# Windowed attention and a dense layer on one core: the two heads of an outer tile side by side in 384 columns, and four blocks for the global queries

## The chip, the core and the metric

The kernel runs on one core of a Trainium2 chip. The metric is the device time of one execution in microseconds (us), the median of several runs. The profile and the trace come from one more execution, which the hardware profiler recorded; its times stand beside its own span and not beside the median. PE is the TensorE matmul engine and PEld its weight load, DVE is VectorE, ACT ScalarE, POOL GpSimd, and SP the SyncE, whose queue issues nearly all DMAs here.

## The reference

For 8 batches of 8 heads with 512 local and 32 global tokens of 64 values, local queries see the global keys and the local keys at most 32 positions away; global queries see all 544 keys. The result goes through a dense layer of 512 to 768 to 512 with the maximum of three products in the middle.

```
out_g = softmax(scale * q_g @ [k_g, k_l].T) @ [v_g, v_l]
s_ll  = where(|i - j| <= 32, scale * q_l @ k_l.T, -1e9)
out_l = softmax([scale * q_l @ k_g.T, s_ll]) @ [v_g, v_l]
x = concat(out_g, out_l) as (8 * 544, 512)
out = maximum(maximum(x @ w1, x @ w2), x @ w3) @ w_out
```

All is float32. Where the kernel needs its exactness at the fast matmul form (float32r), a value is split into a high part (a cast) and a low part (a subtraction), and products of the parts are added.

## The kernel before

The two heads of a pair go together: 8 batches of 4 pairs make 32 pairs (`p`), and each pair has four tiles (`t` = 0 to 3) of 128 local queries, so there are 128 tiles. A tile `sl` = 4p + t sees one window of keys out of a list of 18 groups of 32 (the 16 local ones and twice the global one, `UNITS`): 192 keys for t = 0 and 3, which are the outer tiles, and 224 for t = 1 and 2 (`WIN`).

The loop at L567 handles one tile in each pass, in stages that lie some passes apart: `scores` three tiles ahead (L315: matmuls into PSUM, mask, exponential, division by the sum; the weights `s` then go to the tile `prob` by a DMA, L351, from tile 16 on), `trans` one tile ahead (L354: transposes on PE by an identity into the one PSUM bank `turned`, which the trace calls T, then a copy into `pt`, and from tile 26 on also a subtraction for the low part), and `pv` for the tile itself (L391: matmuls with the values). Between these, `fill(n)` puts in n matmuls of the dense layer for the batch before (`moe_local`, lines L441 and L462), so that PE has work while a tile's softmax passes through DVE, ACT and POOL. At a batch's start `fill(400)` finishes the layer of the batch two back.

Before, `s` and `prob` are laid out as two heads of 256 columns. `trans` makes four transposes: for each head one of 128 keys (L362) and one of the rest, 64 or 96 (L363). The copy reads all 512 columns of T.

Global queries: `glob` (L274) computes the 64 rows of the pair's two heads against 544 keys a pair ahead, `glob_soft` (L297) normalises them into `sg` and sends them in six pieces by DMA (`GPUT`, L303) into `probg`, three blocks of 128 keys. Each tile then transposes one block (`transg`, L381) and copies 64 or 128 of its columns behind the 128 local queries of `pt`, so that the same `pv` matmuls treat them: such a matmul has 160 columns for each of the two parts, 320 in all, in place of 256. With 64 or 128 columns copied, the number of wide matmuls over t = 0, 1, 2, 3 is 2, 4, 2, 4. For pairs 0 to 3 (whose tiles are the first 16, in the order `SEQ`) the global queries come later, in `late` (L496), one pair in the course of every four tiles from 16 to 31; it loads keys and values again into `side`, makes six transposes, multiplies them by a mask `cover`, and adds up twelve small matmuls.

The first 16 tiles (`EARLY`) use plain float32 and the tile `early` without a DMA; the weights of the dense layer are unpacked from their 64-bit form at the same time (`convert`, on ACT, DVE and POOL).

The order on each engine is set by a scheduler, which takes the program in the order in which it is written and moves instructions by their dependences. Which engine does a copy or a subtraction is chosen by `least`, from running sums of estimated costs, so a change in widths can move such work between engines.

Of the kernel before, what the change touches and what calls it, by code (L numbers as in the profile page):

```python
# [33 lines left out]
for _o, _w in WIN:  # L34
# [20 lines left out]
def body(ctx, tc, kin, qin, vin, min_, win, out):  # L55
# [73 lines left out]
    early = const.tile([128, 4, 2, 256], F32, name="early", tag="early")  # L129
# [167 lines left out]
    def glob_soft(p):  # L297
        if p >= B * NP:
            return
        s, nm, z = pg[p]  # L300
        soft(s, nm, z)
        for c0, n, i, h, d0 in GPUT:
            nc.sync.dma_start(out=f32(probg[p % 2])[64 * h:64 * h + 64, i, d0:d0 + n], in_=s[:, c0:c0 + n])  # L303
# [10 lines left out]
    def scores(sl):  # L314
# [26 lines left out]
        for j in range(2):  # L341
            dve.tensor_tensor_reduce(out=s[:, j, 0:n], in0=ph[j][:, 0:n], in1=mask[:, (1, 0, 1, 0)[t], 32 * (t == 0):32 * (t == 0) + n],  # L342
                                     scale=-0.125, scalar=3.0e38, op0=ALU.add, op1=ALU.min, accum_out=nm[:, j:j + 1])
            act.activation(out=s[:, j, 0:n], in_=s[:, j, 0:n], func=AF.Exp, bias=nm[:, j:j + 1], scale=-1.0,  # L344
                           accum_out=z[:, j:j + 1])
        for j in range(2):
            dve.tensor_scalar(out=z[:, j:j + 1], in0=z[:, j:j + 1], scalar1=1e-9, scalar2=None, op0=ALU.add)  # L347
            dve.reciprocal(out=z[:, j:j + 1], in_=z[:, j:j + 1])
            times(s[:, j, 0:n], s[:, j, 0:n], z[:, j:j + 1])
        if sl >= EARLY:  # L350
            nc.sync.dma_start(out=f32(sc[sl])[:, :, 0:n], in_=s[:, :, 0:n])  # L351
        spend("d", 2 * (n * 1.04 + 75) + 150)
        spend("a", 2 * (n * 0.833 + 278))

    def trans(sl):
# [3 lines left out]
        ps, n = turned, WIN[sl % 4][1] - 128  # L359
        pr, ident = (ps, one) if sl < EARLY else (ps.bitcast(F32R), identr)  # L360
        for j in range(2):
            pe.transpose(pr[:, 256 * j:256 * j + 128], s[:, j, 0:128], ident)  # L362
            pe.transpose(pr[0:n, 256 * j + 128:256 * j + 256], s[:, j, 128:128 + n], ident)  # L363
        src = ps.rearrange("p (x q) -> p x q", q=128)
        if sl < NAT:
            pt = pts[sl] = att.tile([128, 2, 2, 160], F32, name="pt", tag="pt")
            copy(pt.rearrange("p j c q -> p (j c) q")[:, :, 0:128], src, True)
        else:
            pt = pts[sl] = att.tile([128, 2, 2, 2, 160], F32R, name="pt", tag="pt")
            v = pt.rearrange("p j c a q -> p (j c) a q")  # L370
            copy(v[:, :, 0, 0:128], src, True)
            sub(v[:, :, 1, 0:128], src, f32(v)[:, :, 0, 0:128], True)

    def transg(sl):
# [4 lines left out]
        i, h, n = GCH[t]  # L379
        g = psS.tile([128, 512], F32, name="S")  # L380
        pe.transpose(g.bitcast(F32R)[:, 0:128], probg[p % 2][:, i], identr)  # L381
# [305 lines left out]
```

## Time and profile before

| | us |
|---|---|
| median of 3 runs | 829.01 |
| lowest and highest of the runs | 828.31, 830.57 |
| the profiled execution's own time | 830.49 |
| its span, first to last instruction | 828.7 |
| PE busy in the span | 803.0 |
| DVE, ACT, POOL busy | 614.8, 510.2, 459.3 |

The profile counts how long each engine was busy and shows by which wait it stood. Matmuls are pipelined: one lasts longer than the distance to the next, so what a PE instruction costs in a dense stretch is read from the starts of its successors in the timeline, not from its duration. On SP, a row is the time in which the queue issues a DMA; the data land later.

### The profile page before, as it was taken

Reading aid. Unit: us, or ns where it says so; the run is one execution under the profiler, and the core shown is the slowest. Engines: PE = TensorE matmul, PEld = TensorE weight load, DVE = VectorE, ACT = ScalarE, POOL = GpSimd, SP = SyncE. Lnnn points to the kernel's source line nnn. Section 1 sums busy time; section 2 is a strip of 40 time slices with the busy share of each in tenths; the row PEclk is TensorE's granted clock in tenths of the full one; section 3 lists DMA queues with packets and bytes.
Section 4 is the critical chain, followed back from the end, with each engine's and each line's share of the span. In section 5 each row is a group of like instructions: output and inputs, shape, how many; then the busy total and the mean of one; then the engine's idle time right before and its main releaser. Section 6 shows DMA issues by size and latency. Waiting matters only on the chain.

```text
span 828.7 us, 16580 instructions
## 1 busy us (share of the span) xinstructions
PE 803.0 (97%) x4772; PEld 683.8 (83%) x4772; DVE 614.8 (74%) x2192; ACT 510.2 (62%) x1416; POOL 459.3 (55%) x623
## 2 busy tenths in 40 slices
PE   6788999999999999999999999999999999999997
PEld 5577888888888888888888888888888888888896
DVE  6999997878887888888887888788887888412111
ACT  5888786666666666666766667676666666311111
POOL 3223355756676667767675676866776665311211
PEclk9989999999999999999999999999999999999999
DMA  8956555533335333443335333443335332100001
GB/s 295 314 178 224 169 152 149 165 116 99 116 108 152 112 97 104 131 136 94 99 104 170 112 98 97 127 139 98 97 96 165 110 100 63 60 13 1 25 27 26
DMA packets 97466, 98.15 MB, mean 118 GB/s; under 512 B 19296, under 2 KB 85856, under 8 KB 97376
## 3 DMA queue, kind: packets, MB, share of 16 engines
q1 hardware_dynamic: 97232, 96.87, 38.0%
q8 instruction: 38, 0.62, 0.3%
q14 instruction: 52, 0.43, 0.2%
q10 hardware_dynamic: 144, 0.23, 0.1%
HBM read 60.39 MB, written 8.91 MB: 84 GB/s over the span
## 4 chain that ended last, share of the span: by engine, by line
PE 80%; DVE 5%; DMA 4%; issue 3%; ACT 3%; POOL 3%; SPq 1%; POOLq 0%; ACTq 0%; DVEq 0%
PE pm L441 45%; PE pm L462 16%; PE O L409 6%; PE S L339 5%; PE T L362 2%; PE T L363 2%; DMA prob<-s 2%; PE S L289 1%; PE S L335 1%; POOL h L103 1%; PE O L401 1%; DMA vraw<-v_in 1%; ACT s L344 1%; PE S L381 1%; DMA raw<-w_in 1%
## 5 line engine op out<-in xcount | busy, mean ns | idle before, releaser
L441 PE MATMUL pm<-xs,w 128*128 128x512 f32 (+1 forms) x2160 | 487.3, 366 | 1.3 <-ACT m L115 0.9
L441 PEld LDWEIGHTS pm<-xs,w 128*128 128x128 f32 x2160 | 354.3, 190 | 52.7 <-issue 4.2
L462 PE MATMUL pm<-w,h 128*128 128x512 f32 x612 | 157.5, 397 | 2.3 <-POOL h L103 2.1
L103 POOL TENSOR_TENSOR h<-m,h 128x512 fp32r<-128x512 f32 (+1 forms) x59 | 70.3, 1192 | 108.5 <-ACT h L115 107.9
L462 PEld LDWEIGHTS pm<-w,h 128*128 128x128 f32 x612 | 109.0, 188 | 23.0 <-POOL h L103 4.4
L450 DVE TENSOR_TENSOR m<-pm,m 128x512 f32<-128x512 f32 (+1 forms) x120 | 72.8, 607 | 66.3 <-PE pm L441 65.6
L103 POOL TENSOR_TENSOR qs<-qraw,qs 128x256 fp32r<-128x256 f32 x100 | 76.7, 767 | 70.4 <-issue 34.8
L344 ACT ACTIVATE s<-s,nm 128x192 f32<-128x192 f32 (+1 forms) x224 | 103.3, 462 | 19.6 <-DVE nm L342 14.1
L125 POOL TENSOR_SCALAR s<-s,z 128x224 f32<-128x224 f32 (+1 forms) x192 | 83.9, 444 | 36.1 <-ACT lox L115 20.4
L342 DVE CUSTOM_DVE_ANT_0 s<-S,mask 128x192 f32<-128x192 f32 (+1 forms) x224 | 74.5, 369 | 15.2 <-PE S L339 7.0
L103 DVE TENSOR_TENSOR pt<-T,pt 128x512 fp32r<-128x512 f32 x102 | 70.4, 690 | 19.4 <-ACT pt L115 18.2
L103 POOL TENSOR_TENSOR vs<-vraw,vs 128x256 fp32r<-128x256 f32 x102 | 75.6, 741 | 12.6 <-ACT vs L115 9.3
L409 PEld LDWEIGHTS O<-pt,vs 128*128 128x128 f32 x408 | 66.2, 188 | 9.9 <-issue 1.6
L409 PE MATMUL O<-pt,vs 128*128 128x320 f32 (+1 forms) x408 | 72.9, 300 | 1.4 <-DVE pt L103 1.4
L339 PEld LDWEIGHTS S<-kst,qs 128*128 128x128 f32 x400 | 59.5, 190 | 8.7 <-DVE nmg L293 0.2
L417 DVE TENSOR_TENSOR xr<-O,lox 64x160 f32<-64x160 f32 x204 | 64.4, 315 | 3.1
L103 POOL TENSOR_TENSOR kst<-kraw,kst 64x576 fp32r<-64x576 f32 x44 | 63.9, 1453 | 4.3 <-DMA prob<-s 1.0
L115 ACT CAST pt<-T 128x512 fp32r<-128x512 f32 x102 | 60.3, 591 | 9.5 <-PE T L363 7.1
L115 ACT CAST qs<-qraw 128x256 fp32r<-128x256 f32 x94 | 38.3, 407 | 44.0 <-PE S L339 28.8
L115 ACT CAST h<-m 128x512 fp32r<-128x512 f32 (+1 forms) x59 | 33.2, 562 | 51.7 <-DVE m L450 51.6
L339 PE MATMUL S<-kst,qs 128*128 128x192 f32 (+1 forms) x400 | 59.5, 270 | 0.0
L347 DVE TENSOR_SCALAR z<-z 128x1 f32<-128x1 f32 x256 | 37.5, 147 | 27.1 <-ACT s L344 17.9
(123 smaller groups left out, 1183.7 us busy)
## 6 DMA issues: line engine op xcount, KB each, us to landing
vraw<-v_in SPq DMA_DIRECT2D x122, 128.0 KB, 2.3
qraw<-q_in SPq DMA_DIRECT2D x100, 128.0 KB, 2.2
prob<-s SPq DMA_DIRECT2D x56, 224.0 KB, 2.5
raw<-w_in SPq DMA_DIRECT2D x24, 512.0 KB, 5.3
prob<-s SPq DMA_DIRECT2D x56, 192.0 KB, 2.3
out_dram<-o SPq DMA_DIRECT2D x32, 256.0 KB, 2.4
kraw<-k_in SPq DMA_DIRECT2D x25, 320.0 KB, 3.1
qn<-q_in SPq DMA_DIRECT2D x29, 128.0 KB, 3.6
```

The lines of the kernel that those rows point to most:

```text
L103: (dve if least(c) == "d" else pool).tensor_tensor(out=out, in0=a, in1=b, op=ALU.subtract)
L115: act.copy(out=out, in_=a)
L125: pool.tensor_scalar(out=out, in0=a, scalar1=col, scalar2=1.0, op0=ALU.mult, op1=ALU.mult)
L339: pe.matmul(ph[j][:, 0:n], lhsT=qs[sl][:, a, 128 * j:128 * j + 128], rhs=kst[p][:, j, c0:c0 + n], start=(a == 0), stop=(a == 1))
L342: dve.tensor_tensor_reduce(out=s[:, j, 0:n], in0=ph[j][:, 0:n], in1=mask[:, (1, 0, 1, 0)[t], 32 * (t == 0):32 * (t == 0) + n], scale=-0.12 ...
L344: act.activation(out=s[:, j, 0:n], in_=s[:, j, 0:n], func=AF.Exp, bias=nm[:, j:j + 1], scale=-1.0, accum_out=z[:, j:j + 1])
L347: dve.tensor_scalar(out=z[:, j:j + 1], in0=z[:, j:j + 1], scalar1=1e-9, scalar2=None, op0=ALU.add)
L409: pe.matmul(o[:, j, 0:320].rearrange("p (a q) -> p a q", a=2)[:, :, 0:n], lhsT=vs[sl][:, 2 * j + c].rearrange("p a d -> p (a d)"), rhs=pt[ ...
L417: dve.tensor_tensor(out=xr[p][64 * j:64 * j + 64, t], in0=o[0:64, j, 0:160], in1=lo[:, j], op=ALU.add)
L441: pe.matmul(ps[:, 0:n], lhsT=weight(3 * f + i, w)[:, 128 * k:128 * k + 128], rhs=xs[k][:, a, c0:c0 + n], start=(q == 0), stop=(q == 11))
L450: dve.tensor_tensor(out=m[:, 0:n], in0=ps[:, 0:n], in1=m[:, 0:n], op=ALU.max)
L462: pe.matmul(ps, lhsT=hh[f][:, a, 128 * t:128 * t + 128], rhs=weight(18 + f, w), start=(q == 0), stop=(q == 17))
```

## The change

Outer tiles keep the weights of the two heads side by side, 192 columns each, so 384 in all. `trans` then makes three transposes of 128: keys 0 to 127 of the first head, the last 64 of the first with the first 64 of the second, and the rest of the second. The values are packed on the host to fit: a head's part of a shared block meets zeros in the other head's rows. `pv` makes as many matmuls as before (four to a tile, or four of the high and low kind); copies and subtractions of `pt` have 384 columns for outer tiles and 512 for inner ones. Inner tiles keep four transposes, in another order of blocks.

`probg` has four blocks, one for each tile, filled by ten DMAs in place of six; seven of the ten have 32 rows, the others 64 as all had before. The number of 32-column pieces copied behind `pt` becomes 3, 4, 2, 3 for the four tiles (96, 128, 64 and 96 columns; before 64, 128, 64 and 128), and the number of wide `pv` matmuls 3, 4, 2, 4. `late` has its own value array `vg` of 640 columns (before 1024 columns of `v`), five transposes in place of six, ten small matmuls in place of twelve, and a plain copy in place of the multiplication by `cover`, which is gone with its six memsets.

```diff
-GPUT = [(0, 128, 0, 0, 0), (128, 96, 1, 0, 32), (224, 96, 1, 1, 0), (320, 64, 0, 1, 64), (384, 96, 2, 0, 32),
-        (480, 64, 2, 1, 0)]
+GPUT = [(0, 32, 0, 128, 0, 0, 0), (32, 32, 0, 64, 0, 32, 64), (32, 32, 64, 64, 0, 64, 0),
+        (0, 64, 128, 96, 1, 0, 32), (0, 64, 224, 96, 1, 64, 0), (0, 64, 320, 64, 2, 0, 64),
+        (0, 32, 384, 96, 3, 0, 32), (0, 32, 480, 64, 3, 32, 0), (32, 32, 384, 32, 3, 32, 96), (32, 32, 416, 128, 3, 64, 0)]
-GCH = [(0, 0, 1), (1, 0, 2), (0, 1, 1), (2, 0, 2)]
+GBL = [3, 4, 2, 3]
...
-        for c0, n, i, h, d0 in GPUT:
-            nc.sync.dma_start(out=f32(probg[p % 2])[64 * h:64 * h + 64, i, d0:d0 + n], in_=s[:, c0:c0 + n])
+        for r0, m, c0, n, i, e0, d0 in GPUT:
+            nc.sync.dma_start(out=f32(probg[p % 2])[e0:e0 + m, i, d0:d0 + n], in_=s[r0:r0 + m, c0:c0 + n])
...
+        if sl >= EARLY and outer(sl):
+            nc.sync.dma_start(out=f32(sc[sl])[:, 0:2 * n], in_=whole[:, 0:2 * n])
...
+    def outer(sl):
+        return sl % 4 in (0, 3)
+    def block(sl, j, c):
+        return j + c if outer(sl) else 2 * c + j
...
-        for j in range(2):
-            pe.transpose(pr[:, 256 * j:256 * j + 128], s[:, j, 0:128], ident)
-            pe.transpose(pr[0:n, 256 * j + 128:256 * j + 256], s[:, j, 128:128 + n], ident)
+        x = 3 if outer(sl) else 4
+        if x == 3:
+            for b in range(3):
+                pe.transpose(pr[:, 128 * b:128 * b + 128], s[:, 128 * b:128 * b + 128], ident)
...
-        g = psS.tile([128, 512], F32, name="S")
-        pe.transpose(g.bitcast(F32R)[:, 0:128], probg[p % 2][:, i], identr)
+        pe.transpose(g.bitcast(F32R)[:, 0:128], probg[p % 2][:, t], identr)
...
+    def wide(t, j, c):
+        return c == 0 or t in (1, 3) or (t == 0 and j == 1)
...
-                    n = 160 if c < GCH[t][2] else 128
+                    b = block(sl, j, c)
+                    n = 160 if wide(t, j, c) else 128
...
-    PARTS = [(0, 0, 0), (1, 0, 96), (1, 1, 224), (2, 0, 256), (3, 0, 352), (3, 1, 480)]
+    PARTS = [0, 128, 256, 384, 416]
...
-        dve.tensor_tensor(out=gt, in0=g[:, 0:384].rearrange("p (x g) -> p x g", g=64), in1=cover.to_broadcast([128, 6, 64]), op=ALU.mult)
+        copy(gt, g[:, 0:320].rearrange("p (x g) -> p x g", g=64), True)
```

The lines of the changed kernel have other numbers: L371 are the three transposes of an outer tile, L393 the transpose of the global block, L338 the scores, L425 the `pv` matmuls, L457 the dense layer; L299 the `probg` DMAs, L350 and L352 the `prob` DMAs of an outer and an inner tile.

On PE, this is one pass of the loop in the middle of the program, with the transposes of an outer tile (T from `prob`), before:

```order
L441 MATMUL pm<-xs,w_396 128x512 x10
L381 MATMUL S<-identr,probg 128x128
L362 MATMUL T<-identr,prob 128x128
L363 MATMUL T<-identr,prob 64x128
L362 MATMUL T<-identr,prob 128x128
L363 MATMUL T<-identr,prob 64x128
L441 MATMUL pm<-xs,w_437 128x512 x4
L339 MATMUL S<-kst,qs 128x224 x4
```

and now:

```order
L457 MATMUL pm<-xs,w_392 128x512 x10
L393 MATMUL S<-identr,probg 128x128
L371 MATMUL T<-identr,prob 128x128 x3
L457 MATMUL pm<-xs,w_432 128x512 x4
L338 MATMUL S<-kst,qs 128x224 x4
```

The neighbours and their counts are the same; three transposes of full width stand where two full and two half ones stood.

On SP, this is the stretch from a `probg` burst to the second `prob` DMA after it, for a pair in the middle of a batch (`prob1` is for the tile with t = 1, `prob0` for t = 2; `sg` is what the burst sends), before:

```order
L227 DMA kraw_6838<-k_in 128x640
L303 DMA probg1_96<-sg_6605 64x128
L303 DMA probg1_96<-sg_6605 64x96 x2
L303 DMA probg1_96<-sg_6605 64x64
L303 DMA probg1_96<-sg_6605 64x96
L303 DMA probg1_96<-sg_6605 64x64
L250 DMA qraw_6829<-q_in 128x256
L351 DMA prob1_94<-s_6727 128x2x224
L265 DMA vraw_6873<-v_in 128x256
L250 DMA qraw_6915<-q_in 128x256
L351 DMA prob0_93<-s_6808 128x2x224
```

and now:

```order
L299 DMA probg0_95<-sg_6942 32x128
L299 DMA probg0_95<-sg_6942 32x64 x2
L299 DMA probg0_95<-sg_6942 64x96 x2
L299 DMA probg0_95<-sg_6942 64x64
L352 DMA prob1_94<-s_7063 128x2x224
L299 DMA probg0_95<-sg_6942 32x96
L299 DMA probg0_95<-sg_6942 32x64
L299 DMA probg0_95<-sg_6942 32x32
L299 DMA probg0_95<-sg_6942 32x128
L246 DMA qraw_7168<-q_in 128x256
L261 DMA vraw_7212<-v_in 128x256
L246 DMA qraw_7254<-q_in 128x256
```

`prob1` now stands behind six `probg` issues, where six and a `qraw` stood before it; the other four, `qraw`, `vraw` and a second `qraw` stand between it and `prob0`.

On SP at the first pair of a batch (where the stores `out_dram` of the dense layer are issued too), before:

```order
L303 DMA probg0_95<-sg_7584 64x128
L303 DMA probg0_95<-sg_7584 64x96 x2
L303 DMA probg0_95<-sg_7584 64x64
L303 DMA probg0_95<-sg_7584 64x96
L303 DMA probg0_95<-sg_7584 64x64
L250 DMA qraw_7817<-q_in 128x256
L265 DMA vraw_7859<-v_in 128x256
L351 DMA prob1_94<-s_7710 128x2x224
```

and now:

```order
L299 DMA probg0_95<-sg_7598 32x128
L299 DMA probg0_95<-sg_7598 32x64 x2
L299 DMA probg0_95<-sg_7598 64x96 x2
L299 DMA probg0_95<-sg_7598 64x64
L299 DMA probg0_95<-sg_7598 32x96
L299 DMA probg0_95<-sg_7598 32x64
L299 DMA probg0_95<-sg_7598 32x32
L352 DMA prob1_94<-s_7723 128x2x224
L299 DMA probg0_95<-sg_7598 32x128
```

Here nine `probg` issues stand before `prob1`, where six, a `qraw` and a `vraw` stood.

More of the change, by code (lines that the diff above doesn't have):

```diff
@@ L128, in body @@
     make_identity(nc, one)
-    early = const.tile([128, 4, 2, 256], F32, name="early", tag="early")
+    early = const.tile([128, 4, 512], F32, name="early", tag="early")
     identr = const.tile([128, 128], F32R, name="identr")
@@ L134, in body @@
     dve.memset(zero, 0.0)
-    prob = [const.tile([128, 2, 256], F32R, name=f"prob{i}") for i in range(2)]
-    probg = [const.tile([128, 3, 128], F32R, name=f"probg{i}") for i in range(2)]
+    prob = [const.tile([128, 512], F32R, name=f"prob{i}") for i in range(2)]
+    probg = [const.tile([128, 4, 128], F32R, name=f"probg{i}") for i in range(2)]
     qgz = const.tile([128, 2, 160], F32R, name="qgz")
-    cover = const.tile([128, 6, 1], F32, name="cover")
     def clear():
-        pool.memset(cover, 1.0)
-        for x, a, n in ((1, 0, 32), (2, 96, 32), (3, 0, 64), (4, 0, 32), (5, 64, 64)):
-            pool.memset(cover[a:a + n, x], 0.0)
         for t in (*probg, qgz):
@@ L322, in scores @@
         else:
-            s = att.tile([128, 2, 224], F32, name="s")
+            s = att.tile([128, 448], F32, name="s")
             sc[sl] = prob[sl % 2]
+        w = n if outer(sl) else 256 if sl < EARLY else n
+        whole = s
+        s = [s[:, w * j:w * j + n] for j in range(2)]
         nm = small.tile([128, 2], F32, name="nm")
@@ L399, in pv @@
             for c, j in ((0, 0), (0, 1), (1, 0), (1, 1)):
-                n = 160 if sl >= EARLY and c < GCH[t][2] else 128
-                pe.matmul(o[64 * j:64 * j + 64, 0, 0:n], lhsT=vraw[sl][:, 2 * j + c], rhs=pt[:, j, c, 0:n], start=(c == 0), stop=(c == 1))
+                b = block(sl, j, c)
+                n = 160 if sl >= EARLY and wide(t, j, c) else 128
+                pe.matmul(o[64 * j:64 * j + 64, 0, 0:n], lhsT=vraw[sl][:, 2 * j + c], rhs=pt[:, b, 0:n], start=(c == 0), stop=(c == 1))
             n = 160 if sl >= EARLY else 128
@@ L661, in _pack @@
                     m[np.abs(d) <= 32, t - 1, 32 * c + i] = 0.0
-    return k, q, v, m
+    once = UNITS[:12] + UNITS[13:]
+    vg = np.concatenate([vt[u][0] for u in once[:16]] + [zero[0]] * 3 + [vt[once[16]][0]], axis=1)
+    vg = np.ascontiguousarray(vg.reshape(NP, 2, 5, 128, D).transpose(0, 3, 2, 1, 4)).reshape(NP, 128, 640)
+    return k, q, v, vg, m
 def _pieces(w1, w2, w3, w4):
```

73 lines of the change are left out of this document (43 added, 30 removed).

## The prediction

> **What bounds the kernel now.** I read the page's busy times first, then stretches of the span, then who waited for whom on PE once the first stage is over.
>
> ```profile
> PE 803.0 (97%) x4772; PEld 683.8 (83%) x4772; DVE 614.8 (74%) x2192; ACT 510.2 (62%) x1416; POOL 459.3 (55%) x623
> ```
> ```profile
> 38.00:42.00 4.00, 1.79 (x16) 1.11 (x15) 4.00 (x13) 3.70 (x10) 0.00 (x0) 1.00 0.88 297
> 42.00:46.00 4.00, 2.78 (x8) 1.74 (x9) 4.00 (x14) 3.20 (x9) 2.21 (x2) 0.54 0.02 6
> 46.00:50.00 4.00, 4.00 (x22) 3.99 (x21) 4.00 (x15) 3.72 (x12) 0.70 (x1) 0.61 0.04 5
> ```
> ```profile
> 125.00:150.00 25.00, 22.62 (x212) 20.41 (x211) 19.65 (x80) 16.33 (x48) 14.10 (x21) 1.00 0.54 155
> ...
> 451.00:543.00 92.00, 91.45 (x515) 77.99 (x513) 76.27 (x275) 61.92 (x173) 63.16 (x88) 1.00 0.39 117
> ...
> 724.00:829.00 105.00, 100.05 (x543) 86.85 (x541) 16.93 (x32) 15.52 (x30) 16.34 (x17) 0.99 0.06 18
> ```
> ```profile
> PE pm L462 <- POOL h L103: 2.1, 4, 0.5
> PE T L362 <- DMA prob<-s: 0.5, 2, 0.3
> ```
>
> A row of the stretches has the start and end, the length, then busy us of PE, PEld, DVE, ACT and POOL, the granted clock, the DMAs' share and their GB/s. There are three stages. Up to about 150 us PE has holes, and DVE is full (4.00 of 4 us in all three short rows): weights are unpacked there. From 180 to 724 us, where the last two rows hold, PE is full; it waits 2.6 us in all. The last 105 us are the dense layer alone, which the change doesn't touch. So an instruction taken from PE in the middle stage is worth its distance to the next one, and work taken from DVE, ACT or POOL there is worth nothing.
>
> **Transposes: the gain.** These are an inner tile's transposes (first one, and the matmul after the fourth), and all rows of an outer tile.
>
> ```profile
> 457.08 0.23 PE L362 MATMUL T<-identr,prob 128*128 128x128 f32 x1
> ...
> 457.37 1.15 PE L441 MATMUL pm<-xs,w 128*128 128x512 f32 x4
> ```
> ```profile
> 462.84 0.22 PE L381 MATMUL S<-identr,probg 128*128 128x128 f32 x1
> 462.89 0.23 PE L362 MATMUL T<-identr,prob 128*128 128x128 f32 x1
> 462.96 0.23 PE L363 MATMUL T<-identr,prob 128*64 128x128 f32 x1
> 463.02 0.24 PE L362 MATMUL T<-identr,prob 128*128 128x128 f32 x1
> 463.10 0.23 PE L363 MATMUL T<-identr,prob 128*64 128x128 f32 x1
> 463.16 1.14 PE L441 MATMUL pm<-xs,w 128*128 128x512 f32 x4
> ```
>
> From first start to the next matmul, four transposes cost 0.27 us in the outer tile (384 columns of weights) and 0.29 in the inner one (448 columns). If that is a fixed part for each of four and a part for each column, 64 columns cost 0.02, the 384 columns 0.12, and the fixed part is (0.27 - 0.12) / 4 = 0.04. Three transposes of 128 then cost 0.27 - 0.04 = 0.23. By the distance after a full-width one (0.07 and 0.08) they cost about 0.22. I take a saving of 0.05 us for each outer tile. The bounds: three at 0.08 save 0.03; three at 0.05, the distance from the global transpose to the next, save 0.12; at columns alone, nothing (a rival below). From tile 32 on there are 48 outer tiles, so 48 x 0.05 = 2.4 us; tiles 16 to 31 have 8, 0.4 us. In the first 16 PE isn't full, and I count that below.
>
> Copies and subtractions of `pt` get shorter by 128 columns on ACT and DVE. In the middle stage that is hidden work, 76.27 and 61.92 busy of 92; worth nothing.
>
> **Wide matmuls: the loss.** A pair has 13 wide `pv` matmuls for 12.
>
> ```profile
> L409 PE MATMUL O<-pt,vs 128*128 128x320 f32 x306 | 66.9, 307 | 1.4 <-DVE pt L103 1.4
> ...
> L409 PE MATMUL O<-pt,vs 128*128 128x256 f32 x102 | 27.6, 279 | 0.0
> ```
>
> The fixed part of a duration is the same in both, so the 64 more columns cost 28 ns, once in each of the 24 pairs from tile 32 on: 0.7 us lost.
>
> **The late global queries.** For one of the four pairs, first its transposes and the next instruction, then its twelve small matmuls (24 instructions, since plain float32 goes in two) and the next:
>
> ```profile
> 101.95 0.58 PE L513 MATMUL S<-one,side 64*128 64x64 f32 x6
> 102.46 0.76 PE L401 MATMUL O<-pt,vraw 128*64 128x160 f32 x8
> ...
> 104.36 0.89 PE L519 MATMUL O<-gt,side 128*64 128x32 f32 x24
> 105.18 0.26 PE L363 MATMUL T<-identr,prob 128*96 128x128 f32 x1
> ```
>
> A transpose costs 0.51 / 6 = 0.09, the matmuls 0.82 / 24 = 0.034 each, and one and four go: 0.22 us a pair, 0.9 in all if PE were full. It idled 2.4 us of 25 in one stretch of this stage, so I take 0.7, between 0 and 0.9.
>
> **The first stage.** There DVE and ACT matter.
>
> ```profile
> L515 DVE TENSOR_TENSOR gt<-S,cover 128x384 f32<-128x384 f32 x4 | 2.2, 546 | 0.0
> ```
> ```profile
> L115 ACT COPY pt<-T 128x512 f32<-128x512 f32 x24 | 14.0, 582 | 4.4 <-PE T L363 4.3
> ...
> L115 ACT COPY xr<-O 128x128 f32<-128x128 f32 x14 | 3.6, 258 | 3.7 <-PE O L401 3.7
> ```
>
> The multiplication by `cover` leaves DVE (2.2 us in all); its copy goes to ACT. 384 columns lie between the two ACT copies, 324 ns, so a copy with 128 fewer is 0.11 us shorter, 1.4 us over the 13 outer tiles before tile 26. But the work that fills DVE around 40 us, the unpacking, stays, and the engines' shares of it shift by one instruction here and there. Bounded by a gain of 2.2 and a loss of as much, I take a gain of 0.3, near nothing.
>
> **The `probg` burst on SP.** This is where the change could give back what it gains: 28 pairs issue four more DMAs, and `prob` is queued behind them.
>
> ```profile
> 465.22 4.89 SPq L303 DMA_DIRECT2D probg<-sg  x6
> 470.21 0.52 SPq L250 DMA_DIRECT2D qraw<-q_in  x1
> 470.85 0.64 SPq L351 DMA_DIRECT2D prob<-s  x1
> ...
> 472.23 0.40 SPq L250 DMA_DIRECT2D qraw<-q_in  x1
> 473.24 0.64 SPq L351 DMA_DIRECT2D prob<-s  x1
> ```
> ```profile
> 473.93 0.22 PE L362 MATMUL T<-identr,prob 128*128 128x128 f32 x1
> ...
> 479.83 0.23 PE L362 MATMUL T<-identr,prob 128*128 128x128 f32 x1
> ```
> ```profile
> L303 SPq DMA_DIRECT2D probg<-sg x168: 462/594/1902, 78.5 to 698.1; - x168
> ```
> ```profile
> prob<-s SPq DMA_DIRECT2D x56, 224.0 KB, 2.5
> ```
>
> A `prob` DMA of an inner tile lands 2.5 us after issue. Here the tile with t = 1 lands at 473.35 for transposes at 473.93, 0.6 us to spare; that with t = 2 lands at 475.74 for 479.83, 4.1 to spare. A `probg` issue takes 0.59 us in the middle. With 32 rows in place of 64 it isn't in the trace; the whole spread, 0.46 to 1.9, has one size, and I take 0.6. In the new order of an ordinary pair, t = 1 stands one `qraw` earlier, a gain of 0.6 us of room. For t = 2, four issues come ahead: 2.4 of its 4.1 us. The first `qraw` behind the burst slips by 3.0 (the four and `prob1`); `next_scores` loads it two passes before it is split, and a pass is 5.8 us (457.08 to 462.89), so it has time. So ordinary pairs lose nothing, and the small wait of 0.5 us in the middle stage may go.
>
> At a batch's first pair it is different:
>
> ```profile
> 533.99 4.76 SPq L303 DMA_DIRECT2D probg<-sg  x6
> ...
> 539.96 0.64 SPq L351 DMA_DIRECT2D prob<-s  x1
> ```
> ```profile
> 543.15 0.25 PE L362 MATMUL T<-identr,prob 128*128 128x128 f32 x1
> ```
>
> Three more issues come ahead (1.8) and a `qraw` and a `vraw` no longer do (538.75, where the burst ends, to 539.96, 1.2 with their gaps): 0.6 us later. This DMA is needed 3.2 us after its issue and takes 2.5 or more, so hardly any room is left. There are five such pairs from tile 48 on (49, 65, 81, 97, 113): between 0 and 3.0 us. I take two of them, 1.2, less the wait of 0.5 that may go and what room there is (0.3): 0.4 us lost.
>
> **The sum.** -2.4 - 0.4 + 0.7 - 0.7 - 0.3 + 0.4 = -2.7 us. For the profiled execution, 830.49 us with a span of 828.7 and 1.8 outside it, that gives 827.8 and a span of 826.0. Runs of before lie from 828.31 to 830.57 with a median of 829.01; from the median, 826.3.
>
> **Rivals.**
>
> *Columns count, not transposes (no change).* The outer tile loads 384 columns before and after. If the load of the weights sets the distance, nothing of 2.8 us is saved and the lost 0.7 stays: 829.0 + 0.1 = 829.1. Against it stand the rows above: 384 and 448 columns differ by a sixth, the times 0.27 and 0.29 by a fourteenth. The Trainium skill has this rule in TensorE: Matmul & The Clock Gate, LDWEIGHTS (loading the stationary operand): the load takes as many steps of a 1.2 GHz clock as the operand has columns, whatever its rows; by it, 384 columns take 320 ns both times and the sum would be this rival's. The 0.27 us measured here for the same 384 columns are less than that, so loads overlap and the rule isn't the distance. 12 in 100.
>
> *The burst eats the gain (no change).* If all five batch starts lose what nine issues cost beyond the two that go (0.6) and ordinary pairs lose 0.05 each where a `prob` lands late, 3.0 + 1.0 in place of 0.4: 829.0 - 2.7 + 3.6 = 829.9. For it: the room of 0.6 and less. Against it: t = 1 stands earlier in all other pairs. 10 in 100.
>
> *The first stage loses its clock once more (slower).* In 38 to 42 us PE idled 2.2 us, and in the next 8 us its granted clock was 0.54 and 0.61, a loss of 0.46 x 4 + 0.39 x 4 = 3.4 us. The new order in the first stage is slightly different on DVE and ACT. If it opens one more such hole, it costs 2.2 + 3.4 = 5.6: 829.0 - 2.7 + 5.6 = 831.9. It decides from about 2 us of idle time in 4. Against it: the orders of DVE and ACT in the first 40 us differ by single instructions. The Trainium skill, same page, Part 1: The HAM clock gate, has the clock halve after an idle window of some 3.4 us; the trace shows it close to half after less idle time. 13 in 100.
>
> *The hole at 40 us closes (faster).* The opposite of the last: 3.4 us come back, 822.9. 5 in 100.
>
> **Chances.** About 0.3% (2.5 us) is what a measurement of this kernel can tell from no change. My forecast, 826.3, has 60 in 100, with its own range of 822.5 to 828.5 from the bounds above (0.03 to 0.12 on a transpose, 0 to 3.0 on SP, 2.2 both ways in the first stage); it lies at the edge of 2.5 us, and since the bounds reach further down than up, 48 of the 60 fall on the faster side. Faster is 48 + 5 = 53, no change 12 + 12 + 10 = 34, slower 13. The range, 822.0 to 831.9, takes in all cases but the ends of each.
>
> **What would show it.** Right: in the timeline an outer tile's three transposes take 0.21 to 0.24 us to the next matmul; 180 to 724 us shrinks by about 2; PE's waits for `prob` stay under 2 us there. Wrong: 0.27 us for three; a wait of PE for `prob` at tiles 49, 65, 81, 97 and 113 or at ordinary t = 1 or 2 of more than 2 us; a clock below 0.9 in new places before 150 us.

## The result, and the profile after

| us | before | after |
|---|---|---|
| median of the runs | 828.66 (4 runs, 828.27 to 830.57) | 839.86 (4 runs, 837.53 to 842.15) |
| the profiled execution, its span | 830.49, 828.7 | 838.89, 837.1 |

The change made the kernel slower: the ratio is 1.013, with a 95% interval of 1.0096 to 1.0165. The medians are 11.2 us apart and the two profiled executions 8.4; the account below is of these 8.4 and leaves the other 2.8 open.

The page's busy times of the changed kernel, and its rows for the stretches (columns as in the prediction):

```profile
PE 806.9 (96%) x4688; PEld 683.0 (82%) x4688; DVE 608.7 (73%) x2187; ACT 504.9 (60%) x1430; POOL 454.0 (54%) x608
```
```profile
38.00:42.00 4.00, 1.76 (x12) 1.03 (x13) 4.00 (x12) 3.42 (x9) 0.00 (x0) 0.81 0.86 301
42.00:46.00 4.00, 3.31 (x11) 2.16 (x11) 3.92 (x15) 3.09 (x10) 1.98 (x2) 0.50 0.00 0
46.00:50.00 4.00, 4.00 (x20) 4.00 (x19) 3.91 (x14) 3.98 (x13) 0.56 (x1) 0.50 0.02 4
```

DVE, ACT and POOL are each about 5 to 6 us less busy, as a narrower `pt` should make them, and the end is later all the same. The hole in PE near 40 us is where it was, and the low clock with it lasts longer: 0.50 from 40.4 to 50.7 us, before from 42.3 to 49.1.

To see where the time goes, one takes an instruction that occurs once in every tile and compares its starts. The transposition of the global block (L381 before, L393 after) is one. These are the rows for tiles 16, 32 and 127 of the kernel before, and then of the changed kernel (minimum, median and longest ns, then the start):

```profile
L381 PE MATMUL S<-identr,probg x1: 308/308/308, 84.8 to 84.8; 128*128 128x128 f32 x1
...
L381 PE MATMUL S<-identr,probg x1: 281/281/281, 176.1 to 176.1; 128*128 128x128 f32 x1
...
L381 PE MATMUL S<-identr,probg x1: 223/223/223, 719.7 to 719.7; 128*128 128x128 f32 x1
```
```profile
L393 PE MATMUL S<-identr,probg x1: 222/222/222, 82.8 to 82.8; 128*128 128x128 f32 x1
...
L393 PE MATMUL S<-identr,probg x1: 226/226/226, 179.7 to 179.7; 128*128 128x128 f32 x1
...
L393 PE MATMUL S<-identr,probg x1: 221/221/221, 728.1 to 728.1; 128*128 128x128 f32 x1
```

Tile 16 is 2.0 us early, tile 32 is 3.6 late, tile 127 8.4 late, and nothing is added after that. The gain at tile 16 isn't the change's: of the kernels below, those that leave the first 32 tiles as they were (e8, e9, e10, e12, e13) start tile 16 1.7 to 2.0 early as well, so the profile of before is a little slow there. Its own rows show the reason, a second hole in PE with a low clock behind it just ahead of tile 16, which those five and the change don't have:

```profile
80.00:84.00 4.00, 1.95 (x13) 1.75 (x14) 3.47 (x10) 2.62 (x9) 0.54 (x1) 0.91 0.29 76
84.00:88.00 4.00, 4.00 (x21) 2.96 (x21) 3.70 (x11) 2.42 (x8) 1.35 (x1) 0.66 0.45 149
```

Tiles 16 to 31 lose about 5 us, and the middle stage, which the prediction took for nearly safe, loses 4.8. (Below, delays are those of the transposition's weight load, which can differ from these by 0.2.)

PE's waits in the middle stage of the changed kernel (total, times, longest, us); the prediction has those of before:

```profile
PE T L374 <- DMA prob<-s: 2.0, 5, 0.9
PE T L371 <- DMA prob<-s: 1.5, 2, 1.0
PE S L338 <- DVE nmg L289: 1.3, 2, 1.0
PE T L374 <- DVE xs L104: 0.8, 1, 0.8
```

The POOL wait of 2.1 us, which came in the last pair of four batches, is gone. In its place the transposes wait 3.5 us for `prob`, before it was 0.5, and scores wait 1.3 us for DVE. The waits for `prob` are at tiles 37, 39, 43, 54, 57, 70 and 109, none of them at a batch's first pair. All listed waits come to 5.6 us against 2.6. The profile counts a wait from the modelled end of the matmul before it; from one start to the next, the steps with a wait exceed the usual step by 8.1 us in all, before by 4.3. That is 3.8 more; less the 0.3 that transposes and wide matmuls save together, it makes 3.5 of the 4.8. The other 1.3 are spread over many steps of the scores and the dense layer, and their cause wasn't found.

The transposes of an outer tile and the next matmul in the timeline of the changed kernel:

```profile
469.30 0.40 PE L371 MATMUL T<-identr,prob 128*128 128x128 f32 x3
469.53 1.16 PE L457 MATMUL pm<-xs,w 128*128 128x512 f32 x4
```

They take 0.23 us, as forecast. What fails lies around them. This is SP of the changed kernel at the same pair as in the prediction, then PE at the tile with t = 1, which waits for the first of these `prob` DMAs, and all `probg` issues of the kernel (least, median and longest ns):

```profile
473.25 3.75 SPq L299 DMA_DIRECT2D probg<-sg  x6
477.11 0.64 SPq L352 DMA_DIRECT2D prob<-s  x1
477.85 2.46 SPq L299 DMA_DIRECT2D probg<-sg  x4
480.41 0.53 SPq L246 DMA_DIRECT2D qraw<-q_in  x1
```
```profile
480.29 0.31 PE L374 MATMUL T<-identr,prob 128*128 128x128 f32 x2
```
```profile
L299 SPq DMA_DIRECT2D probg<-sg x280: 496/588/1603, 79.1 to 711.7; - x140
```

In the same trace an issue with 32 rows takes 0.58 us (the median of 196) and one with 64 rows 0.59 (of 84), and ten with the `prob` between them hold SP for 7.1 us. The burst also starts later: 7.0 us ahead of these transposes (473.25 to 480.29), where it was 8.7 before (465.22 to 473.93). The cause is on POOL; first before, then after:

```profile
464.48 0.71 POOL L125 TENSOR_SCALAR sg<-sg,zg 64x544 f32<-64x544 f32 x1 [1.50 <-ACT pt L115]
465.16 1.30 POOL L103 TENSOR_TENSOR h<-m,h 128x512 fp32r<-128x512 f32 x1
```
```profile
471.23 1.30 POOL L104 TENSOR_TENSOR h<-m,h 128x512 fp32r<-128x512 f32 x1 [1.83 <-DMA vraw<-v_in]
472.51 0.71 POOL L126 TENSOR_SCALAR sg<-sg,zg 64x544 f32<-64x544 f32 x1
```

In the middle stage the scheduler now puts the subtraction for `h` ahead of the multiplication that `sg` needs, in all ordinary pairs. This comes with the layout and not with the widths that are counted: of the kernels below, e5 and e9 have it with the old widths, and e6 with the new ones on the old layout has not.

### The profile page after: what moved, and what is told of

It is laid out like the page before. It is cut to its first block, busy times and chain, and to the rows that moved or that the text cites. A ratio compares the mean times of both kernels' runs of the same rounds, so it can differ in the third digit from the quotient of the medians.

```text
span 837.1 us, 16616 instructions
## 1 busy us (share of the span) xinstructions
PE 806.9 (96%) x4688; PEld 683.0 (82%) x4688; DVE 608.7 (73%) x2187; ACT 504.9 (60%) x1430; POOL 454.0 (54%) x608
## 4 chain that ended last, share of the span: by engine, by line
PE 81%; DMA 6%; DVE 5%; ACT 4%; issue 2%; SPq 1%; POOL 1%; DVEq 0%; ACTq 0%; POOLq 0%
PE pm L457 44%; PE pm L478 16%; PE O L425 6%; PE S L338 5%; DMA prob<-s 4%; PE T L371 2%; PE S L334 2%; PE S L285 1%; PE T L374 1%; PE O L416 1%; DMA qn<-q_in 1%; PE T L376 1%; SPq L299 1%; ACT s L343 1%; PE S L393 1%
## 5 line engine op out<-in xcount | busy, mean ns | idle before, releaser
L457 PE MATMUL pm<-xs,w 128*128 128x512 f32 (+1 forms) x2160 | 487.5, 366 | 0.8 <-DVE xs L104 0.5
L457 PEld LDWEIGHTS pm<-xs,w 128*128 128x128 f32 x2160 | 354.6, 190 | 51.7 <-issue 4.5
L126 POOL TENSOR_SCALAR s<-s,z 128x224 f32<-128x224 f32 (+1 forms) x183 | 80.0, 444 | 37.1 <-ACT lox L116 17.8
L104 DVE TENSOR_TENSOR pt<-T,pt 128x512 fp32r<-128x512 f32 (+1 forms) x102 | 63.3, 621 | 18.2 <-ACT pt L116 16.7
L425 PE MATMUL O<-pt,vs 128*128 128x320 f32 (+1 forms) x408 | 73.6, 302 | 1.2 <-DVE pt L104 1.2
L425 PEld LDWEIGHTS O<-pt,vs 128*128 128x128 f32 x408 | 66.1, 188 | 9.9 <-issue 1.4
L338 PEld LDWEIGHTS S<-kst,qs 128*128 128x128 f32 x400 | 59.0, 190 | 12.3 <-DVE nmg L289 4.4
L116 ACT CAST qs<-qraw 128x256 fp32r<-128x256 f32 x77 | 31.3, 407 | 52.6 <-PE S L338 29.4
L338 PE MATMUL S<-kst,qs 128*128 128x192 f32 (+1 forms) x400 | 60.1, 272 | 1.4 <-DVE nmg L289 1.3
L116 ACT CAST pt<-T 128x512 fp32r<-128x512 f32 (+1 forms) x102 | 55.0, 540 | 9.7 <-PE T L376 4.4
```

Source lines behind the costliest of these rows:

```text
L104: (dve if least(c) == "d" else pool).tensor_tensor(out=out, in0=a, in1=b, op=ALU.subtract)
L116: act.copy(out=out, in_=a)
L126: pool.tensor_scalar(out=out, in0=a, scalar1=col, scalar2=1.0, op0=ALU.mult, op1=ALU.mult)
L338: pe.matmul(ph[j][:, 0:n], lhsT=qs[sl][:, a, 128 * j:128 * j + 128], rhs=kst[p][:, j, c0:c0 + n], start=(a == 0), stop=(a == 1))
L425: pe.matmul(o[:, j, 0:320].rearrange("p (a q) -> p a q", a=2)[:, :, 0:n], lhsT=vs[sl][:, 2 * j + c].rearrange("p a d -> p (a d)"), rhs=pt[ ...
L457: pe.matmul(ps[:, 0:n], lhsT=weight(3 * f + i, w)[:, 128 * k:128 * k + 128], rhs=xs[k][:, a, c0:c0 + n], start=(q == 0), stop=(q == 11))
```

## The experiments

All kernels were run beside the kernel before on one chip in each group. The table has each run's median and ratio with its interval, and from its trace the delay of tiles 32 and 127 against the profile of before; "middle" is the difference of the two. A profiled execution can lie a few us from its kernel's median, mostly by its first stage: e8, e9, e10, e12 and e13 leave that as it was and lie from -1.8 to -0.2 there. So the middle is the safer measure. Part of that scatter is the granted clock, which drops to 0.50 for 3.4 us or a multiple. Ahead of tile 32 the profiled execution has 6.8 us of it in e4, e6 to e10 and e12, 10.2 us in the kernel before, in the change and in e13, and 13.7 us in e1, e2, e3, e5 and e11. By our estimate 3.4 us at half clock cost up to half of that, 1.7, so up to 1.7 of the delay of tile 32 in these last five, against before, is the clock of that one execution. From tile 32 to 127 the clock is 1.00 in all of them.

| kernel | us | ratio (95%) | tile 32 | tile 127 | middle |
|---|---|---|---|---|---|
| the change | 839.86 | 1.0130 (1.0096 to 1.0165) | +3.4 | +8.4 | +5.0 |
| e1_before_ten | 835.37 | 1.0057 (1.0037 to 1.0076) | +6.0 | +6.2 | +0.2 |
| e2_after_six | 834.63 | 1.0057 (1.0036 to 1.0079) | +7.8 | +8.5 | +0.7 |
| e3_after_later | 838.67 | 1.0097 (1.0072 to 1.0123) | +5.9 | +8.9 | +3.0 |
| e4_after_dve | 836.33 | 1.0078 (1.0049 to 1.0107) | +3.3 | +5.9 | +2.6 |
| e5_after_old_costs | 833.58 | 1.0052 (1.0029 to 1.0075) | +6.9 | +6.6 | -0.3 |
| e6_before_new_costs | 831.76 | 1.0028 (1.0010 to 1.0047) | +0.4 | +1.3 | +0.9 |
| e7_before_late | 832.11 | 1.0034 (1.0013 to 1.0055) | +1.7 | +1.5 | -0.2 |
| e8_ten_from_pair_8 | 829.84 | 1.0005 (0.9983 to 1.0027) | -1.3 | -1.3 | 0.0 |
| e9_middle_old_costs | 830.98 | 1.0022 (1.0001 to 1.0044) | -1.1 | +0.3 | +1.4 |
| e10_middle_new_costs | 836.52 | 1.0081 (1.0053 to 1.0108) | -0.6 | +3.5 | +4.1 |
| e11_other_constant | 834.90 | 1.0066 (1.0046 to 1.0085) | +3.3 | +4.9 | +1.6 |
| e12_qs_on_act | 832.41 | 1.0032 (1.0013 to 1.0051) | -1.8 | +1.0 | +2.8 |
| e13_middle_six | 830.20 | 1.0009 (0.9990 to 1.0027) | -0.2 | -0.2 | 0.0 |

### The burst and where it stands: four runs

The first theory was that the ten issues on SP cost it all. The kernel before, with its six pieces cut into ten (`GPUT` has ten entries):

```diff
-        for c0, n, i, h, d0 in GPUT:
+        for r0, m, c0, n, i, h, d0 in GPUT:
```

> The kernel before with its six probg pieces sent as ten (three of 64 rows, or two, left whole, the others cut into two of 32 rows; same bytes to the same places, four blocks of issues more on SP, nothing else changed). Theory burst (the four more issues on SP hold up prob and qraw, so PE waits): it is as slow as the change or slower, since it has no shorter transposes: 836 to 843 us, PE's waits for prob 5 to 8 us. Theory layout (the 384 columns, the other order of the prob and pt blocks, or what POOL does because of them, costs the time; issues are hidden): 827 to 830, as before.

The loss is there, 4.7 us by the ratio, but all of it ahead of tile 32. The engines in the stretch from 60 to 120 us, which takes in tiles 16 to 22, before and in this run:

```profile
60.00:120.00 60.00, 57.47 (x447) 47.95 (x446) 57.38 (x203) 48.11 (x145) 21.42 (x19) 0.97 0.58 183
```
```profile
60.00:120.00 60.00, 55.05 (x416) 44.54 (x415) 54.78 (x194) 45.46 (x133) 18.44 (x18) 0.97 0.57 176
```

PE and DVE, both near full before, are 2.4 and 2.6 us less busy in these 60 us, with the same work to do: it comes to them later. The middle stage takes four more issues a pair for nothing.

The changed kernel without the four pieces of the fourth block:

```diff
-        for r0, m, c0, n, i, e0, d0 in GPUT:
+        for r0, m, c0, n, i, e0, d0 in GPUT[:6]:
```

> The changed kernel with six of its ten probg pieces: the four of the fourth block (the global queries' keys for tiles with t = 3) are left out, so that the fourth block stays zero; everything else is as in the change. Theory burst: all of the loss goes and the gain of three transposes less the one more wide matmul shows: 825 to 829. Theory layout: 836 to 842, as the change.

With six issues the middle stage of the changed kernel is nearly whole again (+0.7), though the planner (`least` with its running sums) shares out the work in the new way; the first stage stays late. Then the last four pieces one pass later, past the `prob` of t = 2:

```diff
-        for r0, m, c0, n, i, e0, d0 in GPUT:
+        send(p, GPUT[:6])
...
+                send(p + 1 if i >= 16 else 4, GPUT[6:])
```

> The changed kernel with the four pieces of the fourth block issued one pass later in the program (at t = 3 in place of t = 2). Same number of issues. Theory burst: the stretches of ten in a row go, a qraw comes between in ordinary pairs and the first stage has prob behind six: the loss of 3.6 us before tile 32 goes and part of the rest: 831 to 836. Theory number (what counts is the sum of SP's issue time, not how they are bunched): 837 to 842. Theory layout: 837 to 842.

That saves 2 of the 5 us in the middle and little as a whole. The fourth run takes the multiplication for `sg` from POOL, where it stands behind `h`:

```diff
-        times(s, s, z[:, 0:1])
+        dve.tensor_scalar(out=s, in0=s, scalar1=z[:, 0:1], scalar2=None, op0=ALU.mult)
```

> The changed kernel with the division of the global weights sg by their sum always on DVE, in place of nearly always on POOL (0.56 for 0.74 us, and not behind POOL's other work). In the changed kernel that multiplication starts 1.6 us later against the transposes than before, and the burst with it. Theory burst with a late start: the burst begins 1.5 to 2 us earlier and 3 to 6 us come back: 833 to 837. Theory burst, but its length alone: 837 to 842.

This halves the loss of the middle stage. The multiplication takes 1.14 us on DVE in the mean, not the expected 0.56. The edit also leaves it out of the planner's sums, and DVE does 11 copies into `qs` in place of the change's 18 (below), so the run doesn't show the place of the burst alone. So the burst matters in the middle, but only along with something that the kernel before doesn't have.

### What the planner makes of the narrower tiles: three runs

`least` adds estimated times by width, so a `pt` of 384 columns makes an engine look freer. The changed kernel with the old widths counted, and `late`'s copy kept on DVE:

```diff
-            copy(pt[:, 0:x, 0, 0:128], src, True)
+            copy(pt[:, 0:x, 0, 0:128], src, True, 512)
...
-        copy(hi, src, True)
+        copy(hi, src, True, (64, 128, 64, 128)[t])
```

> The changed kernel, but the planner that hands copies and subtractions to engines counts pt's blocks with the widths of before (512 columns, and 64 or 128 for the global ones), and the copy of the late queries stands on DVE where the product with the mask stood. So the engines get the shares of before; the work itself and the ten issues are those of the change. Theory shares (the first stage loses its 3.4 us because ACT, DVE and POOL got other pieces of it): those come back, 833 to 836. Theory burst for the first stage as well: 837 to 841, with the loss before tile 32 still there.

PE's waits in its middle stage:

```profile
PE T L374 <- DMA prob<-s: 0.4, 2, 0.2
PE S L338 <- DVE nmg L289: 0.3, 1, 0.3
PE T L371 <- DMA prob<-s: 0.3, 1, 0.3
```

The loss of 5 us in the middle is gone with all ten issues in place, and with POOL's `h` still ahead of `sg`: that order alone costs nothing either. The first stage, whose loss the expectation hoped to get back, is later still (+6.9). Which work the widths move shows in the groups of ACT and DVE for the whole middle stage. First before, then the change:

```profile
L115 ACT CAST qs<-qraw 128x256 fp32r<-128x256 f32 x87 | 35.4, 407 | 41.5 <-PE S L339 27.5 <-issue 7.8 <-POOL kst L103 1.7
...
L113 DVE CAST qs<-qraw 128x256 fp32r<-128x256 f32 x3 | 1.1, 352 | 0.0
```
```profile
L116 ACT CAST qs<-qraw 128x256 fp32r<-128x256 f32 x73 | 29.7, 407 | 51.8 <-PE S L338 29.4 <-DMA qraw<-q_in 12.1 <-issue 4.1
...
L114 DVE CAST qs<-qraw 128x256 fp32r<-128x256 f32 x18 | 11.8, 654 | 0.3 <-DMA qraw<-q_in 0.2
```

Some fifteen copies into `qs` went from ACT, 407 ns each, to DVE, where the planner counts 283 ns (256 x 0.52 + 75 + 75) and the trace has 654 (the last section shows why). ACT also waits 12.1 us for `qraw`, which it does not do before; but it waits 15.1 in this run with the old widths, whose middle stage loses nothing, so that wait is not the cost. The two parts by themselves, on the kernel before: the new widths, and the new `late`.

```diff
-            copy(v[:, :, 0, 0:128], src, True)
+            copy(v[:, :, 0, 0:128], src, True, (384, 512, 512, 384)[sl % 4])
```

> The kernel before, but the planner counts pt's blocks with the widths of the change (384 columns for outer tiles; 96, 128, 64, 96 for the global ones). Nothing that is done changes but which engine does a copy, and the order that follows. Theory shares: the first stage loses 3 us or more by this alone: 831 to 834. Theory burst: 828 to 830.

```diff
-        nc.sync.dma_start(out=v, in_=vin[4 * p:4 * p + 4].rearrange("t p x -> p t x"))
+        nc.sync.dma_start(out=side[:, 640:1280], in_=vgin[p])
...
-        dve.tensor_tensor(out=gt, in0=g[:, 0:384].rearrange("p (x g) -> p x g", g=64), in1=cover.to_broadcast([128, 6, 64]), op=ALU.mult)
+        copy(gt, g[:, 0:320].rearrange("p (x g) -> p x g", g=64), True)
```

> The kernel before with the change's late global queries alone: their own values array of 640 columns, five transposes for six, ten small products for twelve, a copy for the product with the mask, and no cover. By the prediction's own term 0.7 us less: 827 to 829. Theory fragile first stage (any change of what is ready when there gives a worse order than the one it has): 831 to 834, all of it before tile 32. Theory burst: 827 to 829.

The new widths alone put 16 `qs` copies on DVE too and cost 0.9 us in the middle, so they aren't enough. The new `late`, with less to load and to compute, brings no gain: 2.6 us slower by the medians, none of it in the middle.

### The first stage held as it was: six runs

In the kernel before, six issues up to pair 7 and ten from pair 8 on:

```diff
+        if p >= 8:
+            for r0, m, c0, n, i, h, d0 in GTEN:
```

> The kernel before, whose six probg pieces are cut into ten from pair 8 on only (tiles 32 and later; the first stage issues six as before; the output is the same). Theory A, more issues hurt only where the first stage is short of transfers (the kernel before with ten everywhere lost all of its 6 us ahead of tile 32): no delay at tile 32, and under 1 us at the end, 829 to 831 us. Theory B, each of the 24 pairs pays some 0.2 us for four more issues: a delay that grows evenly, 833 to 835 us.

No loss. Then the kernel before up to tile 31, and all of the changed layout from tile 32 on, with the old (e9) and with the new widths (e10) counted (`NEW` is 32, `transn` and `GPUTN` are those of the change):

```diff
+        if sl >= NEW:
+            return transn(sl)
...
+        if 4 * p >= NEW:
+            for r0, m, c0, n, i, e0, d0 in GPUTN:
```

> The kernel before up to tile 31, and from tile 32 on the changed layout (three transposes, four blocks, ten issues, one more wide matmul a pair) with the planner counting the old widths; at pairs 8 and 9 GpSimd clears probg once more, and the output is the same. Theory A, the layout is free in the middle stage when the planner's order stays, and the loss in the first stage belongs to the order there: transposes -1.1, wide matmuls +0.7, no delay at tile 32, 828.5 to 830.5 us. Theory B, the layout or its ten issues cost by themselves wherever they run: 832 to 836 us.

> As the kernel before up to tile 31 with the changed layout from tile 32 on, but the planner counts the changed widths as the change does; the output is the same. Theory A, the new widths put GpSimd's subtraction for the hidden layer ahead of its multiplication for sg and with it the ten issues 1.65 us later: waits of the transposes for prob come up in the middle stage, 2.5 to 5 us behind the run that counts the old widths, 832 to 835 us. Theory B, these waits came from what the first stage left behind (another phase of the engines at tile 32): as with the old widths, 828.5 to 830.5 us.

Between these two lie 5.5 us of the medians, and the one difference is what the planner is told. The runs of e10 go from 833.97 to 841.13, and the profiled one is at their lower end, so its trace (2.7 us behind e9 in the middle stage) shows less than the medians do. PE's waits in the middle stage, old widths and new:

```profile
PE T L394 <- DVE xs L110: 0.8, 1, 0.8
PE T L394 <- DMA prob<-s: 0.8, 2, 0.4
PE pm L524 <- POOL h L110: 0.4, 1, 0.4
```
```profile
PE S L358 <- DVE nmg L302: 1.7, 5, 0.4
PE T L394 <- DMA prob<-s: 1.7, 5, 0.5
PE pm L524 <- POOL h L110: 0.4, 1, 0.4
```

and DVE's copies into `qs` with the new widths:

```profile
L120 DVE CAST qs<-qraw 128x256 fp32r<-128x256 f32 x17 | 13.3, 783 | 0.5 <-DMA qraw<-q_in 0.5
```

From this kernel with the new widths, two runs each take one thing away: the `qs` copies stay on ACT (e12, the first two lines), or the four pieces of the fourth block aren't sent (e13).

```diff
+            if s >= NEW:
+                act.copy(out=t[:, 0], in_=r)
...
+            for r0, m, c0, n, i, e0, d0 in GPUTN[:6]:
```

> The kernel with the changed layout from tile 32 on and the new widths in the planner (836.5 us when run without this edit), with one thing held: the first copy of each qs from tile 32 on stays on ScalarE, where the planner with old widths puts 87 of 90 and with new widths only 73 (a qs copy takes 407 ns there and 783 ns on VectorE). The output is the same. Theory A, VectorE took these copies because its count got smaller, and they hold up the chains that end in prob: 830.5 to 832.5 us, as with old widths. Theory B, GpSimd's order (the subtraction for h ahead of the multiplication for sg) with ten issues is enough: 835 to 837 us.

> The kernel with the changed layout from tile 32 on and the new widths in the planner (836.5 us), without the four pieces of the fourth block from pair 8 on: six issues a pair as before. It leaves out the global keys of the tiles with t=3 from tile 32 on. Theory A, the new shares need the ten issues to hurt (the kernel before with the new widths and six issues lost under 1 us behind tile 32): 831 to 832.5 us. Theory B, the new shares with the new layout hurt whatever is issued: 834.5 to 837 us.

Without the four issues nothing is lost; with the copies on ACT, 4.1 of the 5.5 us come back by the medians, and 1.3 of 2.7 by the profiled executions; PE's wait for `nmg` falls from 1.7 to 0.4 us. PE's waits for `prob` in the middle stage without the four issues (e13), and those for `prob` and for `pt` with the copies on ACT (e12):

```profile
PE T L394 <- DMA prob<-s: 0.4, 2, 0.2
```
```profile
PE T L398 <- DMA prob<-s: 1.6, 4, 1.1
PE T L398 <- DVE pt L110: 1.2, 1, 1.2
```

Two single things in e12 make up 2.3 of its waits, so its profile is a poor measure, and the medians decide. The loss in the middle stage is thus a product. SP's four more issues with the old shares cost nothing in e8 and e5 and 1.4 us in e9, which is 1.3 us slower than before by the medians; the new shares with six issues cost 0.0 to 0.9 (e13, e2, e6); both together cost 4.1 in e10 and 5.0 in the change.

Last, a test of the first stage: the kernel before with one constant of the planner altered.

```diff
-        c = {"a": n * 0.833 + (80 if psum else 110) + k}
+        c = {"a": n * 0.833 + (90 if psum else 110) + k}
```

> The kernel before, with one constant of the planner altered: a copy out of PSUM by ScalarE is counted 10 ns dearer. Nothing else is changed; other engines take some of the work and the order differs. Theory A, before's order in the first stage is an uncommonly good one and almost any other costs: 831 to 834 us, all of it ahead of tile 32. Theory B, the first stage takes such changes of order without loss, and the changed kernel's 4 us there are due to its own parts: 828.5 to 830 us.

An edit that computes, moves and sends just the same costs 5.2 us by the medians; in its trace 3.3 of 4.9 lie ahead of tile 32 and 1.1 more within that tile's pass, up to 1.7 of them by the clock. All nine kernels that alter the first stage are late at tile 32, by 0.4 (e6) to 7.8 us (e2). So the order that the kernel before has there is a good one, and a loss as large as the change's can come from another order alone; that the change's own loss comes from this and nothing else isn't shown.

How the product comes about can be read in part from the room that `prob` has, from its landing to the weight load of the first transpose that needs it; the medians over the 24 tiles of each kind from tile 32 on, in us:

| | t = 1 | t = 2 (least) | t = 3 (least) |
|---|---|---|---|
| before, six issues | 1.5 | 4.1 (3.8) | 1.1 (0.0) |
| e8, ten issues, old shares | 1.2 | 2.9 (1.4) | 1.3 (0.0) |
| e9, layout, ten, old shares | 0.6 | 1.5 (0.0) | 1.5 (0.0) |
| e10, layout, ten, new shares | 0.3 | 1.1 (0.0) | 1.5 (0.0) |
| e13, layout, six, new shares | 0.4 | 3.9 (3.0) | 1.5 (0.0) |
| the change | 0.4 | 1.3 (0.0) | 1.3 (0.0) |

Ten issues use up t = 2's room, and the layout takes most of t = 1's even with six. But of the 3.5 us that the changed kernel waits for `prob`, t = 2 has only 0.7 (tiles 54 and 70), t = 1 has 1.3 (37, 57 and 109) and t = 3 has 1.5 (39 and 43), whose room by the median is no smaller than before. So the table explains the smaller part of the waits. The longest of them, at tile 43 (t = 3), on SP and then on PE:

```profile
235.50 2.26 SPq L246 DMA_DIRECT2D qraw<-q_in  x1
237.93 0.48 SPq L350 DMA_DIRECT2D prob<-s  x1
```
```profile
239.16 0.37 PE L371 MATMUL T<-identr,prob 128*128 128x128 f32 x2 [1.01 <-DMA prob<-s]
```

A `qraw` issue took 2.26 us in place of 0.4 to 0.5 and held the `prob` behind it. The kernel before has ten SP issues of over 1 us in its middle stage, the changed one six, so it isn't their number; whether the kernel before would have had room for this one wasn't tested. By which way the `qs` copies on DVE bring `prob` later, whether through the mask's reduction in front of the exponential or through `sg`, was not followed further. Which part of the change decides in the first stage stays open too: ten issues alone, six issues with the new layout, and a constant alone all lose there.

No version beats the kernel before. The nearest that does all of the change's work, e9, is the layout as it was meant, from tile 32 on with the old shares, and it is still 1.3 us slower.

## Why the prediction was wrong, point by point

**The transposes: right in kind, too large in the sum.** The single rows gave 0.23 us for three, as forecast, against 0.27 for four: 0.04 saved. Summed from start to start over the middle stage, with waits left out, all transposes of `prob` together took 1.0 us less (1.1 in e9), some 0.02 us for each of 48 outer tiles where 0.05 was taken and 0.03 was the lower bound. Full-width transposes in a row stand 0.07 to 0.08 apart. Of 2.4 us of gain 1.0 was there. The rival by which the columns alone count would have saved nothing. The Trainium skill's rule behind it (TensorE: Matmul & The Clock Gate, LDWEIGHTS) gives 320 ns for 384 columns; three transposes of 128 took 0.23 us, so as a distance between transposes the trace goes against it again.

**The wide matmuls: right.** By the same sums the wide ones took 3.5 us more and the narrow ones 2.8 less, 0.7 as forecast.

**The shorter copies: the step that failed.** "In the middle stage that is hidden work, ... worth nothing" was true of the engines' time and false of the planner: its sums got smaller with the widths, and it used the time that DVE had gained to give it `qs` copies. These are the stretches from 180 to 700 us, before, with the old widths (e9) and with the new (e10); the third busy time is DVE's:

```profile
180.00:700.00 520.00, 517.34 (x2904) 441.86 (x2903) 430.45 (x1549) 353.36 (x980) 356.94 (x493) 1.00 0.38 113
```
```profile
180.00:700.00 520.00, 517.50 (x2853) 439.86 (x2852) 418.55 (x1545) 346.96 (x977) 356.48 (x492) 1.00 0.37 112
```
```profile
180.00:700.00 520.00, 515.82 (x2836) 437.32 (x2835) 430.02 (x1545) 346.06 (x981) 350.53 (x481) 1.00 0.37 112
```

DVE saves 12 us by the layout, and with the new widths spends them again, partly on copies that are slower there. With ten issues behind it, that is the 5.5 us between e9 and e10. That a change in widths can move such work was said of the kernel; its price was taken as zero.

**The burst on SP: the other half of that step.** The issue's cost with 32 rows (0.59, taken as 0.6) was right, and t = 2 lost 2.8 of its 4.1 us where 2.4 were forecast. "t = 1 ... a gain of 0.6 us of room" was wrong: it fell from 1.5 to 0.4. POOL's order had not been looked at: t = 1 has 0.3 to 0.8 us in every run with POOL's new order, six issues or ten, and 0.8 to 1.5 in those with the old one. "So ordinary pairs lose nothing" was wrong with it, since all waits for `prob` were in ordinary pairs, while the five batch starts, costed at 0.4, had none. "It has time", of the `qraw` behind the burst, was wrong as well, since ACT waits 12.1 us for it in the middle stage, but e5 waits longer there and loses nothing.

**The first stage: out of its bounds.** A gain of 0.3 with 2.2 both ways was given for tiles 0 to 31. Tile 32 came 3.4 late, some 4 to 5 against the runs that leave the stage alone, of which up to 1.7 is the longer low clock. The bounds came from the amount of work that moved, and e11 shows that the order alone can cost more than these bounds; which of the two did it in the change stays open. The 0.4 and the 0.7 forecast for tiles 16 to 31 and for `late` aren't to be seen in this; e7 has `late` alone, and it lost.

**The rivals.** The one that was slower, a second hole with a low clock, did not happen in the profiled execution: ahead of tile 32 the clock stands at 0.50 for 10.2 us in one piece, and before it did for 10.2 us in two, 6.8 and 3.4. The second hole that the rival feared is one that the kernel before had itself, near 82 us. The runs e1, e2, e3, e5 and e11 have 3.4 us more, so up to 1.7 us of the delay in their traces is this rival's. "The burst eats the gain" named the right queue but priced it at 0.05 a pair; it was 0.2 (5.0 over 24), and only with the new shares.

## What to carry to other kernels

Where a planner shares out work by estimated costs, an edit that makes hidden work shorter is also an edit of the planner's input: see what it moves, and price the moved work by the trace, or hold the old costs and run both. A queue's room should be counted together with the room of whoever fills it, since four more issues were free with one order and cost 5 us with another. Before a loss in a stage is put down to a part of an edit, a run with the order shaken by something harmless shows how much that stage loses to any new order.

## What the runs showed of the hardware

- A cast from SBUF to SBUF of 128x256 took 401 to 408 ns on ACT, as the mean of a group in each kernel, and on DVE 352 (`qs`) to 1155 (`vs`) in the kernel before alone. What lengthens it on DVE is POOL. In the fifteen traces 106 such casts of `qs` and `vs` started on DVE while POOL stood idle, and each took 277 to 297 ns, close to the 283 that the planner counts. Of 457 that started while POOL ran, 440 took over 300 ns, and 338 of these ended 0.13 to 0.17 us behind the end of a POOL instruction, as here in the changed kernel (243.63 after 243.48):

```profile
242.07 0.71 POOL L126 TENSOR_SCALAR sg<-sg,zg 64x544 f32<-64x544 f32 x1
242.61 1.02 DVE L114 CAST vs<-vraw 128x256 fp32r<-128x256 f32 x1
242.75 0.73 POOL L104 TENSOR_TENSOR qs<-qraw,qs 128x256 fp32r<-128x256 f32 x1
```

  The Trainium skill (SBUF — State Buffer, Who interferes with whom) has casts on DVE, in the modes that use two ports, contend with GpSimd for a shared pair of ports, where the one that comes second waits for the whole instruction of the other; these times on DVE and the lack of scatter on ACT agree.
- A DMA issue on SP takes nearly the same time whether its piece has 32 or 64 rows: for `probg` 594 ns in the median of 168 with 64 rows before, 594 of 84 with 64 rows and 582 of 196 with 32 rows after.
- Ten of some 450 SP issues in the middle stage of the kernel before take 1.3 to 1.9 us in place of about 0.5; seven of them are for `probg`. What makes them long is not known.
- The granted clock falls to half in steps of 3.4 us, not only at a full stop: in the 3.4 us ahead of each of the 27 falls before tile 32 in these traces, PE was busy for 24% to 63%.
